# Stores on another issuing queue, the last two query tiles loaded a batch ahead and weighted by ScalarE, attention tiles at odd slots, one token sum later

## The chip, the cores and the metric

The kernel runs on one core of a Trainium2 chip. The metric is device microseconds of one execution. A profiled execution gives a span of its own, about 2 us shorter than the timed median (before: span 314.5 us, median 316.5 us), so spans are compared with spans and medians with medians.

## The reference

Linear attention with a cosine weighting feeds a gated feed-forward block (FFN):

```python
# 8 batches, 8 heads, 576 positions, head size 64
r   = max(x, 0); phi(x) = concat[r * cos(theta_s), r * sin(theta_s)]      # for q and k
kv  = einsum('bhsf,bhsd->bhfd', phi(k), v);  z = phi(k).sum(axis=2)
att = (phi(q) @ kv) / (phi(q) . z + 1e-6)                                 # 4608 tokens x 512
out = (silu(att @ w_gate) * (att @ w_val)) @ w_out                        # d_ff = 1536, float32 out
```

## The kernel before: the parts that matter

The tokens are worked off in nine groups (0 to 8) of 512. A group has 16 slots: twelve blocks of the FFN, then four of the output product. TensorE runs through these in order; everything else (the attention of the next batch, loads, transposes, stores) is hung into slots behind the TensorE work. Groups 7 and 8 (`GATE`) use a seven-product scheme for the gate, groups 2 to 8 for the output; such a scheme needs sums of operands, made by VectorE (`token_sum`, S1 to S4). A few more names: a bank is an accumulation buffer that TensorE writes; m and b are two partial products of the gate's scheme, which VectorE adds; C11 to C22 are the quarters of the output; an attention tile is made by matmuls of phit and kv and then three VectorE steps, den, rec and x.

```python
rel  = ctx.enter_context(tc.tile_pool(name="rel", bufs=1))     # r_q: ONE buffer
rawq = ctx.enter_context(tc.tile_pool(name="rawq", bufs=3))    # q as loaded
obp  = ctx.enter_context(tc.tile_pool(name="obp", bufs=2))     # output tiles
...
def phi_q(b, g):                        # relu on ScalarE, both weights in one multiply on VectorE
    if g == 0:
        st[b, "q"] = rel.tile([P, G, NC, 2, D], BF16, name="r_q")
    o = raws[b, "q"][:, g]
    relu_op("act", o, o)
    nc.vector.tensor_tensor(out=st[b, "q"][:, g], in0=o.unsqueeze(2).to_broadcast([P, NC, 2, D]),
                            in1=tab, op=ALU.mult)

def qturn_dma(b, e):                    # r_q is transposed by two DMA transposes into phit
    if e == 0:
        phit[b] = phip.tile([P, 2, G, NC, SH], BF16, name="phit")
    nc.sync.dma_start_transpose(out=phit[b][:, e]..., in_=st[b, "q"][e * SH:(e + 1) * SH]...)

def x_turn(t):                          # activations of an attention tile, also by DMA transpose
    nc.sync.dma_start_transpose(out=xT_of(t), in_=st["x", t])

def store(t, cols=slice(0, d_model), queues=None):
    for e in range(2):                  # two stores a tile, both on SyncE
        (queues or (nc.sync, nc.sync))[e].dma_start(out=out_v[...], in_=ob_of(t)[e * SH:(e + 1) * SH, cols])

def load_behind(b):                     # GpSimd loads a batch once phit of the one before is there
    nc.gpsimd.tensor_copy(out=hold2, in_=phit[b - 1][0:1, :, 0, 0, 0])
    load(b, "q")
    if b > 3:
        load_kv(b)
...
for b in range(2, B):                   # the plan: batch b is prepared in group b-2 and b-1
    s0 = SLOTS * (b - 1); p0 = s0 - SLOTS
    steps  = [lambda: phi_q(b, g) for g in range(G)]
    steps += [lambda: (relu_k(b, g, g + 1, keng), vmul(b, g)) for g in range(G)]
    fs, tq = [p0 + 12, p0 + 12] + [p0 + 11 + i for i in range(2, 8)], (p0 + 15, p0 + 16)
    at(p0 + 3 if b < 5 else p0 + 1, lambda: load_behind(b))
    ...
for t in ...:                           # the four attention tiles of the next group: their slots
    s = SLOTS * (tg - 1) + ((1, 2, 7, 9) if tg < 6 else (1, 2, 4, 7) if tg < 8 else (1, 2, 5, 6))[i]
    at(s, lambda: a_tile2(t), turn(t))  # (if tg - 1 in GATE)
```

Of the kernel before, what the change touches and what calls it, by code (L numbers as in the profile page):

```python
# [11 lines left out]
BF16 = mybir.dt.bfloat16  # L12
# [6 lines left out]
def kernel(  # L19
# [10 lines left out]
    nc = tc.nc  # L30
    B, H, S, D = q.shape
    P = 128
# [16 lines left out]
    HT = T // 2  # L49
    HD = d_model // 2  # L50
    KH = KC // 2
    GATE = (7, 8)

    consts = ctx.enter_context(tc.tile_pool(name="consts", bufs=1))
# [222 lines left out]
    def phi_q(b, g):  # L277

        if g == 0:
# [3 lines left out]
        nc.vector.tensor_tensor(out=st[b, "q"][:, g], in0=o.unsqueeze(2).to_broadcast([P, NC, 2, D]),  # L283
                                in1=tab, op=ALU.mult)

    def vmul(b, g):
        nc.vector.tensor_tensor(  # L287
            out=v2s[b == 1][:, g, :, :, 0:D],
            in0=(first if b == 0 and g == 0 else {"v": raw_of(b, "v")})["v"][:, g].unsqueeze(2).to_broadcast([P, NC, 2, D]),
            in1=tab, op=ALU.mult,  # L290
        )
# [59 lines left out]
    def kv_out2(b):  # L351

        ps = st[b, "kvps"][:, :, 0:4 * J * D1 // 2].rearrange("p e (j w x) -> p e j w x", j=J, w=2)
        for w, eng in enumerate((nc.scalar.copy, nc.vector.tensor_copy)):
            for i in range(2):
                eng(out=kv2s[b % 2][w * D:(w + 1) * D, :, :, i], in_=ps[i * D:(i + 1) * D, :, :, w])

# [249 lines left out]
    def ffn_by_quarters(tg, slot_of):  # L607

        B11, B12, B21, B22 = x_parts(tg)
        val, gates, count = {}, {}, [0]  # L610

        def bank(nm, **kw):
            return take(1, ("g", tg, nm), **kw).rearrange("p (i x) -> p i x", i=2)

        def free(nm):
            give_back(("g", tg, nm))

        def product(to, u, a, x, first):
            for i in range(2):
                for c in range(KH):  # L620
                    nc.tensor.matmul(out=to[:, i], lhsT=a[:, c, 2 * u + i], rhs=x[:, :, c],  # L621
                                     start=first and i == 0 and c == 0, stop=c == KH - 1, skip_group_check=True)

        def silu(u, w, j, src):
            if (u, w) not in gates:
                gates[u, w] = sg2p.tile([P, 2, T], BF16, name="sg2")
            nc.scalar.activation(out=gates[u, w][:, :, j * HT:(j + 1) * HT], in_=src, func=AF.Silu, scale=DOWN)  # L627

        def V(u, i, w):
            fc = 4 * u + 2 * i + w  # L630
            val[u, i, w] = take(1, ("v", tg, fc), fills=True)
            for kc in range(KC):
                nc.tensor.matmul(out=val[u, i, w], lhsT=wv_sb[:, kc, fc * P:(fc + 1) * P], rhs=xT[tg][:, :, kc],  # L633
                                 start=(kc == 0), stop=(kc == KC - 1))

        def mul(u, i, w):
            fc = 4 * u + 2 * i + w
            nc.vector.tensor_tensor(out=ht[:, fc], in0=gates[u, w][:, i], in1=val.pop((u, i, w)), op=ALU.mult)  # L638
            give_back(("v", tg, fc))

        def done():
            slot_of(count[0])
            count[0] += 1

        for u in range(3):
            a = bank("a", fills=True)
            product(a, u, A11, B11, True)
            b = bank("b", seeded=True)
            nc.scalar.copy(out=b, in_=a)
            e = bank("e", fills=True)  # L650
            product(e, u, W3, X3, True)
            m7 = m7p.tile([P, 2, HT], FP32, name="m7")
            nc.scalar.copy(out=m7, in_=e)
            free("e")
            V(*((u - 1, 1, 1) if u else (u, 0, 0)))
            done()
            product(b, u, W2, X2, False)
            c = bank("c", seeded=True)
            nc.vector.tensor_tensor(out=c, in0=m7, in1=b, op=ALU.add)
            product(a, u, A12, B21, False)  # L660
            silu(u, 1, 0, a)
            free("a")
            if u:
                mul(u - 1, 1, 1)
            V(u, 0, 0) if u else V(u, 1, 0)
            done()
            product(b, u, W1, X1, False)
            nc.vector.tensor_tensor(out=m7, in0=m7, in1=b, op=ALU.add)
            silu(u, 0, 1, m7)
            product(c, u, A22, X4, False)  # L670
            silu(u, 0, 0, c)
            free("c")
            V(u, 1, 0) if u else V(u, 0, 1)
            done()
            if u == 2:
                for n in (1, 2):
                    token_sum(n, 0, 4)
            mul(u, 0, 0)
            mul(u, 1, 0)
            if u == 2:  # L680
                token_sum(3, 4, 6)
            product(b, u, W4, B22, False)
            silu(u, 1, 1, b)
            free("b")
            if u:
                V(u, 0, 1)
            mul(u, 0, 1)
            if u:
                done()
                token_sum(*((3, 0, 4) if u == 1 else (4, 0, 4)))  # L690
        V(2, 1, 1)
        mul(2, 1, 1)
        for n in (1, 2):
            token_sum(n, 4, 6)
        done()
# [12 lines left out]
    def store(t, cols=slice(0, d_model), queues=None):  # L708
        for e in range(2):
            idx = 2 * t + e  # L710
            (queues or (nc.sync, nc.sync))[e].dma_start(out=out_v[idx // NC, idx % NC][:, cols],
                                                        in_=ob_of(t)[e * SH:(e + 1) * SH, cols])
# [40 lines left out]
    def token_sum(n, lo, hi):  # L753
        o, x, y, op = {
            3: (S3, aq[:, 0, 0], aq[:, 0, 1], ALU.subtract),
            1: (S1, aq[:, 0, 1], aq[:, 1, 1], ALU.add),
            2: (S2, S1, aq[:, 0, 0], ALU.subtract),
            4: (S4, aq[:, 1, 0], S2, ALU.subtract),
        }[n]
        nc.vector.tensor_tensor(out=o[:, lo:hi], in0=x[:, lo:hi], in1=y[:, lo:hi], op=op)  # L760
# [6 lines left out]
    def out_by_quarters(tg, slot_of):  # L767

        last = tg == NTG - 1
        t0 = tg * OUT  # L770
        for t in (t0, t0 + 2):
            ob_of(t)
# [41 lines left out]
        product(b, S2, T2, False)  # L814
        for p_, o_, x_ in each(b, c[0], C22):
            nc.vector.scalar_tensor_tensor(out=o_, in0=x_, scalar=UP, in1=p_, op0=ALU.mult, op1=ALU.add)
        token_sum(4, 4, 6)
        slot_of(0)
        product(a, aq[:, 1, 0], bq[:, 1, 0], False)
        copied("act", C11, a)  # L820
# [12 lines left out]
        if last:  # L833
            store_two(t0 + 2, slice(0, HD))
        else:
            for t in (t0 + 2, t0 + 3):
                store(t)
        slot_of(2)
        product(b, S4, bq[:, 1, 1], False)
        copied("dve", C12, b)  # L840
        free("b", nb)
        for t in (t0, t0 + 1):
            store(t, *((slice(HD, d_model), (nc.sync, nc.scalar)) if last else ()))
        slot_of(3)


# [149 lines left out]
    def load_behind(b):  # L996

        nc.gpsimd.tensor_copy(out=hold2, in_=phit[b - 1][0:1, :, 0, 0, 0])  # L998
        load(b, "q")
        if b > 3:  # L1000
            load_kv(b)

    def load_kv(b):
        for nm in ("k", "v"):
# [13 lines left out]
    for b in range(2, B):  # L1018
        s0 = SLOTS * (b - 1)
        keng = "dve" if b == 2 else "act"  # L1020
        steps = [lambda b=b, g=g: phi_q(b, g) for g in range(G)]
        steps += [lambda b=b, g=g: (relu_k(b, g, g + 1, keng), vmul(b, g)) for g in range(G)]
        if b == 2:
            fs, tq = [s0 + i for i in (0, 0, 1, 1, 4, 5, 5, 6)], (s0 + 2, s0 + 2)
        else:
            p0 = s0 - SLOTS
            fs, tq = [p0 + 12, p0 + 12] + [p0 + 11 + i for i in range(2, 8)], (p0 + 15, p0 + 16)
            if b == 3:
                fs, tq = [p0 + 12 + i for i in range(4)] + [s0 + 4, s0 + 4, s0 + 5, s0 + 5], (s0 + 2, s0 + 2)
            at(p0 + 3 if b < 5 else p0 + 1, lambda b=b: load_behind(b))  # L1030
        tk = (s0 + 4, s0 + {2: 8, 3: 7}.get(b, 5))
        for s, f in zip(fs, steps):
            at(s, f)
        for e in range(2):
            at(tq[e], lambda b=b, e=e: qturn_dma(b, e))
        at(tk[-1], lambda b=b: kv_mm(b), lambda b=b: kv_out2(b))
        at(tk[-1] + 1, lambda b=b: kv_free(b))
    for t in range(2 * OUT, NTG * OUT):
        tg, i = divmod(t, OUT)
        s = SLOTS * (tg - 1) + (5 if tg > 2 else 4) + 2 * i  # L1040
        if t == 2 * OUT:
            at(s, a_(t, 0))
            at(s + 1, a_(t, 1), turn(t))
        elif tg == 2:
            at((9, 10, 11)[i - 1] + SLOTS, lambda t=t: a_tile2(t), turn(t))
            if i == 2:
                at(11 + SLOTS, load_3)
        else:
            if t in (13, 14, 15):
                s = SLOTS * 2 + t - 4  # L1050
            elif tg - 1 in GATE:
                s = SLOTS * (tg - 1) + ((1, 2, 7, 9) if tg < 6 else (1, 2, 4, 7) if tg < 8 else (1, 2, 5, 6))[i]
            at(s, lambda t=t: a_tile2(t), turn(t))
    for tg in range(1, NTG):
        s0 = SLOTS * tg
# [46 lines left out]
```

## Time and profile before

| | before |
|---|---|
| timed, median (4 runs) | 316.53 us (316.38 to 317.22) |
| profiled span | 314.5 us |
| TensorE busy | 307.5 us (98%) |
| start of group 1 (first gate product) | 53.84 us |
| groups 1 to 8, us | 33.68, 32.62, 32.39, 32.74, 32.39, 32.43, 30.87, 29.00 |
| last matmul to end | 4.52 us |

A group's length is the distance of the first gate products of two neighbouring groups in the trace, so a wait at a group's start counts in the group before. Where this document says in which group time went, it compares these lengths.

### The profile page before, as it was taken

The page shows a single profiled execution, that of the slowest core. Times are in us where ns is not written, and L with a number is a line of the kernel's source. Part 1 is how long each engine was busy: PE and PEld are TensorE (multiplying, and loading weights), DVE is VectorE, ACT ScalarE, POOL GpSimd, SP SyncE. Part 2 cuts the span into 40 slices and gives each one's busy share as a digit, 9 for nine tenths or more (in the row PEclk, how much of TensorE's full clock was granted, in tenths as well). Part 3 has the DMA queues.
Part 4 walks back from the last instruction along what each step waited for, and adds up shares of the span by engine and source line. Part 5 has one row for each costly group of instructions (what it writes and reads, how often), then busy time and mean ns, then how long its engine had stood idle before and what let it go on. Part 6 is the DMA issues. An engine that isn't in the chain of part 4 may idle for free.

```text
span 314.5 us, 6775 instructions
## 1 busy us (share of the span) xinstructions
PE 307.5 (98%) x2696; PEld 189.7 (60%) x2696; DVE 228.2 (73%) x458; ACT 143.4 (46%) x264; POOL 36.0 (11%) x62
## 2 busy tenths in 40 slices
PE   8899999999999999999999999999999999999994
PEld 4597455455444585548654764577456866687673
DVE  7873777697678888587748786778779478946772
ACT  7554545763335346334543454335533345324530
POOL 7855102000200200030003000300000000000000
PEclk9999999999999999999999999999999999999999
DMA  7999999996897994989495979598951160014004
GB/s 268 217 198 197 206 205 138 226 133 99 143 208 114 150 145 110 148 119 196 100 153 75 200 144 154 73 192 135 164 86 35 40 145 17 20 38 98 0 2 133
DMA packets 74767, 41.07 MB, mean 131 GB/s; under 512 B 49904, under 2 KB 69872, under 8 KB 74736
## 3 DMA queue, kind: packets, MB, share of 16 engines
q1 hardware_dynamic: 51952, 22.55, 38.0%
q0 software_dynamic: 22192, 17.57, 37.2%
q10 hardware_dynamic: 592, 0.52, 0.5%
q8 instruction: 21, 0.34, 0.4%
q14 instruction: 10, 0.08, 0.1%
HBM read 37.75 MB, written 9.44 MB: 150 GB/s over the span
## 4 chain that ended last, share of the span: by engine, by line
PE 91%; DVE 5%; ACT 2%; issue 1%; ACTq 0%
PE banks L564 46%; PE banks L786 20%; PE banks L729 6%; PE banks L633 5%; PE banks L621 5%; PE banks L333 3%; PE banks L448 3%; DVE ht L638 1%; PE banks L494 1%; PE banks L430 1%; DVE v L287 1%; DVE sums L760 1%; DVE x L471 1%; PE banks L197 1%; PE banks L536 0%
## 5 line engine op out<-in xcount | busy, mean ns | idle before, releaser
L564 PE MATMUL banks<-xT,wg_sb 128*128 128x512 f16 (+2 forms) x368 | 86.6, 360 | 0.0
L564 PE MATMUL banks<-xT,wv_sb 128*128 128x512 f16 (+2 forms) x368 | 86.6, 360 | 0.0
L570 ACT ACTIVATE sg<-banks 128x512 bf16<-128x512 f32 (+2 forms) x92 | 51.5, 560 | 76.0 <-PE banks L564 74.0
L575 DVE TENSOR_TENSOR ht<-sg,banks 128x512 f16<-128x512 bf16 (+2 forms) x92 | 57.9, 637 | 29.7 <-PE banks L564 22.7
L564 PEld LDWEIGHTS <-wv_sb 128*128 128x128 f16 x368 | 35.5, 98 | 37.4
L564 PEld LDWEIGHTS <-wg_sb 128*128 128x128 f16 x368 | 33.9, 98 | 31.5 <-issue 0.2
L786 PEld LDWEIGHTS <-ht 128*128 128x128 f16 x336 | 32.5, 98 | 4.2
L786 PEld LDWEIGHTS <-sums 128*128 128x128 f16 x252 | 24.5, 98 | 4.2 <-issue 0.8
L633 PE MATMUL banks<-xT,wv_sb 128*128 128x512 f16 x96 | 24.3, 379 | 0.0
L283 DVE TENSOR_TENSOR r_q<-raw_q,tab 128x1152 bf16<-128x1152 bf16 x24 | 17.6, 754 | 7.4 <-ACT raw_q L266 7.1
L729 PE MATMUL banks<-wo_sb,ht 128*128 128x512 f16 x96 | 22.7, 379 | 0.0
L471 DVE TENSOR_TENSOR x<-banks,rec 128x512 f16<-128x512 f32 (+1 forms) x32 | 21.6, 674 | 1.3 <-PE banks L430 0.3
L786 PE MATMUL banks<-wo_sb,ht 128*128 128x256 f16 x168 | 20.6, 273 | 0.0
L287 DVE TENSOR_TENSOR v<-raw_v,tab 128x1152 bf16<-128x1152 bf16 x27 | 19.9, 751 | 0.5 <-ACT raw_v L849 0.5
L786 PE MATMUL banks<-wt_sb,sums 128*128 128x256 f16 x168 | 19.8, 273 | 0.1
L786 PE MATMUL banks<-wt_sb,ht 128*128 128x256 f16 x168 | 19.5, 273 | 0.0
L799 ACT ACTIVATE ob<-banks 128x512 f32<-128x512 f32 x14 | 8.4, 597 | 21.9 <-PE banks L786 21.9
L638 DVE TENSOR_TENSOR ht<-sg,banks 128x512 f16<-128x512 bf16 x24 | 15.5, 681 | 2.4 <-ACT sg L627 2.4
L266 ACT ACTIVATE raw_k<-raw_k 128x576 bf16<-128x576 bf16 (+1 forms) x25 | 17.1, 694 | 0.0
L998 POOL COPY hold<-phit 1x2 bf16<-1x2 bf16 x5 | 1.4, 287 | 129.3 <-DMA phit<-r_q 129.3
L760 DVE TENSOR_TENSOR sums<-ht 128x1024 f16<-128x1024 f16 (+1 forms) x28 | 15.5, 553 | 0.4
L266 ACT ACTIVATE raw_q<-raw_q 128x576 bf16<-128x576 bf16 x24 | 15.4, 675 | 0.0
(121 smaller groups left out, 334.6 us busy)
## 6 DMA issues: line engine op xcount, KB each, us to landing
out_dram<-ob SPq DMA_DIRECT2D x67, 128.0 KB, 2.5
raw_k<-in_k_dram POOLq DMA_DIRECT2D x7, 576.0 KB, 8.8
raw_q<-in_q_dram POOLq DMA_DIRECT2D x6, 576.0 KB, 6.0
raw_v<-in_v_dram POOLq DMA_DIRECT2D x6, 576.0 KB, 11.4
wo_sb<-in_moe_w_out_dram POOLq DMA_DIRECT2D x3, 512.0 KB, 12.8
wg_sb<-in_moe_w_gate_dram POOLq DMA_DIRECT2D x5, 256.0 KB, 9.4
wv_sb<-in_moe_w_val_dram POOLq DMA_DIRECT2D x5, 256.0 KB, 9.5
wo_sb<-in_v_dram SPq DMA_DIRECT2D x2, 576.0 KB, 4.0
```

The source lines that it names most:

```text
L266: nc.scalar.activation(out=out, in_=in_, func=AF.Relu)
L283: nc.vector.tensor_tensor(out=st[b, "q"][:, g], in0=o.unsqueeze(2).to_broadcast([P, NC, 2, D]), in1=tab, op=ALU.mult)
L287: nc.vector.tensor_tensor(out=v2s[b == 1][:, g, :, :, 0:D], in0=(first if b == 0 and g == 0 else {"v": raw_of(b, "v")})["v"][:, g].unsquee ...
L471: nc.vector.tensor_tensor(out=st["x", t].rearrange("p (y e d) -> p e y d", e=2, d=D)[:, :, ys], in0=ps[:, :, 0:2 * J * D1].rearrange("p e ...
L564: nc.tensor.matmul(out=st["f", tg, fc, lo][i], lhsT=(wg_sb, wv_sb)[i][:, kc, fs], rhs=xT[tg][:, ts, kc], start=(kc == 0), stop=(kc == KC - 1))
L570: nc.scalar.activation(out=sg[:, 0:n], in_=st["f", tg, fc, lo][0], func=AF.Silu, scale=DOWN)
L575: nc.vector.tensor_tensor(out=ht[:, fc, r:r + n], in0=st.pop(("s", tg, fc, lo))[:, 0:n], in1=ps[1], op=ALU.mult)
L633: nc.tensor.matmul(out=val[u, i, w], lhsT=wv_sb[:, kc, fc * P:(fc + 1) * P], rhs=xT[tg][:, :, kc], start=(kc == 0), stop=(kc == KC - 1))
L638: nc.vector.tensor_tensor(out=ht[:, fc], in0=gates[u, w][:, i], in1=val.pop((u, i, w)), op=ALU.mult)
L729: nc.tensor.matmul(out=o_ps[t], lhsT=ht[:, fc, r:r + P], rhs=wo_sb[:, fc], start=(fc == 0), stop=(fc == FC - 1))
L760: nc.vector.tensor_tensor(out=o[:, lo:hi], in0=x[:, lo:hi], in1=y[:, lo:hi], op=op)
L786: nc.tensor.matmul(out=to[i][:, 0] if len(to) == 2 else to[0][:, i], lhsT=a[:, kc, i * P:(i + 1) * P], rhs=b[:, kc], start=first and kc == ...
```

## The change

The intent: SyncE's queue, which carries the transposes TensorE depends on, is freed of stores; q of batches 6 and 7 is loaded a batch ahead, so that it can be turned earlier; VectorE is relieved of weighting it; and VectorE sums that sit just ahead of a TensorE product are moved away from it.

```diff
+    PHI_ACT = 6
+    def phi_q_part(b, c, w):                          # relu(x * w) = relu(x) * w, w = cos or sin >= 0
+        if (b, "q") not in st:
+            st[b, "q"] = rel.tile([P, G, NC, 2, D], BF16, name="r_q")
+        nc.scalar.activation(out=st[b, "q"][:, :, c, w], in_=raws[b, "q"][:, :, c], func=AF.Relu,
+                             scale=csk[:, c, w:w + 1])
 ... ffn_by_quarters: the last sum of the gated groups goes behind the output's start
-                token_sum(*((3, 0, 4) if u == 1 else (4, 0, 4)))
+            if u == 1:
+                token_sum(3, 0, 4)
 ... out_by_quarters
+        queues = (nc.gpsimd, nc.gpsimd) if tg > 2 else None
-        token_sum(4, 4, 6)
+        token_sum(4, 0 if tg in GATE else 4, 6)
-                store(t)
+                store(t, queues=queues)               # and the second pair of stores alike
 ... load_behind
-        load(b, "q")
+        if b < PHI_ACT:
+            load(b, "q")
         if b > 3:
             load_kv(b)
+        if PHI_ACT <= b + 1 < B:
+            load(b + 1, "q")
 ... the plan
-        steps = [lambda b=b, g=g: phi_q(b, g) for g in range(G)]
+        steps = [lambda b=b, g=g: phi_q(b, g) for g in range(G)] if b < PHI_ACT else []
+            if b >= PHI_ACT:
+                for c in range(NC):
+                    at(p0 + 4 + c, lambda b=b, c=c: (phi_q_part(b, c, 0), phi_q_part(b, c, 1)))
+                fs, tq = [p0 + 12, p0 + 12, p0 + 13, p0 + 15], (p0 + 13, p0 + 13)
 ... the attention tiles' slots
-            elif tg - 1 in GATE:
-                s = SLOTS * (tg - 1) + ((1, 2, 7, 9) if tg < 6 else (1, 2, 4, 7) if tg < 8 else (1, 2, 5, 6))[i]
+            elif tg in GATE:
+                s = SLOTS * (tg - 1) + ((1, 3, 7, 9) if tg < 6 else (1, 3, 5, 7))[i]
```

More of the change, by code (lines that the diff above doesn't have):

```diff
@@ L353, in kv_out2 @@
         ps = st[b, "kvps"][:, :, 0:4 * J * D1 // 2].rearrange("p e (j w x) -> p e j w x", j=J, w=2)
-        for w, eng in enumerate((nc.scalar.copy, nc.vector.tensor_copy)):
+        for w, eng in enumerate((nc.scalar.copy, nc.scalar.copy if b - 1 in GATE else nc.vector.tensor_copy)):
             for i in range(2):
@@ L842, in out_by_quarters @@
         for t in (t0, t0 + 1):
-            store(t, *((slice(HD, d_model), (nc.sync, nc.scalar)) if last else ()))
+            store(t, *((slice(HD, d_model), (nc.sync, nc.scalar)) if last else (slice(0, d_model), queues)))
         slot_of(3)
```

## The prediction

> **What bounds the kernel now.** I read the engine shares and the chain that ended last on the profile's page, then TensorE's waits, then the timeline around the stages that the change touches.
>
> ```profile
> PE 307.5 (98%) x2696; PEld 189.7 (60%) x2696; DVE 228.2 (73%) x458; ACT 143.4 (46%) x264; POOL 36.0 (11%) x62
> PE 91%; DVE 5%; ACT 2%; issue 1%; ACTq 0%
> 54.00:310.00 256.00, 255.34 (x2153) 157.21 (x2150) 189.64 (x353) 112.90 (x201) 12.68 (x21) 1.00 0.67 115
> ```
>
> The third line is the stretch view from 54 to 310 us (columns: PE, weight loads, DVE, ACT, POOL, granted clock, DMA share): TensorE is busy for 255.34 of 256.00 us at full clock. It is the bound, so ACT (112.9) or DVE (189.6) work is worth nothing in itself; only TensorE's gaps are. A busy share can hide small ones, so I took the distance of neighbouring matmul starts in the trace less the streaming time of the columns (213 ns for 512, seen all through the FFN, in proportion for fewer). After 100 us the gaps over 60 ns are: 0.20 us before the last output product of each of groups 2 to 5; 0.12 us at 185.28, the start of group 5; in group 7 0.51 (257.20), 0.24 (267.65), some 0.15 (263 to 265) and 0.24 us (274.84); 0.13 us at 303.68 in group 8; and pairs of 0.10 us where the small attention matmuls begin and end, which no reordering removes. **All that this change could win is some 2.3 us, 0.7%.** The program order confirms that no TensorE instruction is added or dropped; five attention tiles only move.
>
> **What the skill says.** (1) The Trainium skill, "ScalarE: Activation LUTs", section "What ACT_TABLE_LOAD costs": an activation takes 186 ns plus 0.833 ns an element, some 93 ns more for a per-partition pointer operand, and neighbours overlap by 93 ns. The trace agrees: 675 ns for 576 columns (formula 666), 475 ns for 260 columns with a pointer scale (496). (2) "DMA: Bandwidth & Descriptors", section "Issuing engines are not separate DMA queues": another issuing engine only saves sequencer time; the 16 DMA engines are shared. (3) The same page, section "SWDGE vs HWDGE vs iDMA": GpSimd's and SyncE's transfers feed different queues of each DMA engine, which takes turns. The trace agrees: activation transposes that land 2.4 us after issue with nothing beside them (255.47 to 257.91) take 8 to 9 us while GpSimd's loads run (203.25 to 211.84).
>
> **The change, part by part.**
>
> Stores on GpSimd: 40 stores (groups 3 to 7) leave SyncE, where a group's eight held the queue 5 to 6 us. GpSimd's issues cost 0.74 us each, 30 us in 190, on an engine idle otherwise. An output buffer is wanted some 25 us later. Directly worth 0. Indirectly, the transpose of r_q no longer waits behind stores.
>
> ScalarE weighting (batches 6 and 7): four relus (675 ns) and four DVE multiplies (754 ns) go; 18 activations of 256 columns with a pointer scale come. Each: 186 + 93 + 213 = 0.49 us, 0.40 us in a row; the traced 475 ns less overlap gives 0.38. A pair costs 0.85 us a slot. With the SiLU (0.60 us) that is 1.45 of the 1.73 us that TensorE spends on a slot. In total ACT gains 2 x (18 x 0.40 - 2.7) = 9 us and DVE loses 6 us, beside TensorE. The multiplies' places before the output's last product are filled by three v multiplies of the same length, so the 0.20 us gaps stay.
>
> Token sum S4 moved behind the output's start: 0.68 us of DVE leaves the front of the S2 sum, for which TensorE waits 0.24 and 0.13 us: -0.37 us.
>
> Tiles at odd slots: in group 7 the second of two neighbouring tiles leaves slot 2, where TensorE waited for its bank:
>
> ```profile
> 256.46 0.69 DVE L471 TENSOR_TENSOR x<-banks,rec 128x512 f16<-128x512 f32 x1
> 257.20 0.60 PE L621 MATMUL banks<-kvt,wgs_sb 128*128 128x256 f16 x4 [0.35 <-DVE x L471]
> ```
>
> But at slots 3 and 7 its 1.1 us of DVE (den 0.17, rec 0.20, x 0.69) stands just before the sum of m and b that TensorE needs two products later. By hand this leaves some 0.3 us a time. Of 0.90 us of gaps I take 0.4 as saved.
>
> q a batch ahead: q of 6 goes behind group 3's loads, some 3.4 us more transfer (k to v there: 146.36 to 149.78), ending near 153.2. That group's last activation transposes landed at 149.99 and 150.58, with the loads; they would now land near 153.5 to 154, and group 4 (152.54) wants them: about 1 us. In group 4 load and transposes start earlier, which frees the 0.12 us at 185.28.
>
> **The wait that I expect to decide.** r_q has one buffer. ScalarE may write batch 6 into it only when both transposes of batch 5 have read it; in the new program the first of the 18 waits for them. It stands after group 4's fifth SiLU:
>
> ```profile
> 152.44 0.76 DVE L283 TENSOR_TENSOR r_q<-raw_q,tab 128x1152 bf16<-128x1152 bf16 x1 [1.26 <-ACT raw_q L266]
> 157.79 7.62 SPq L306 DMA_TRANSPOSE phit<-r_q  x2
> 160.57 0.60 ACT L570 ACTIVATE sg<-banks 128x512 bf16<-128x512 f32 x1 [1.19 <-PE banks L564]
> 167.89 0.42 PE L448 MATMUL banks<-kv,phit 128*128 128x65 bf16 x8
> 169.65 0.18 POOL L998 COPY hold<-phit 1x2 bf16<-1x2 bf16 x1 [31.01 <-DMA phit<-r_q]
> ```
>
> r_q of batch 5 is full at 153.20; its transposes start at 157.79, behind the stores, and are done at 169.5, 11.7 us later (10.1 to 12.0 us over the five pairs). ScalarE would be there at 161.2. Without stores ahead the pair starts at 153.3, and ends at L = 165.0; sharing the DMA engines with the group's stores, now on the other queue (a store is 64 packets of 2 KB at 115 ns, 0.46 us of 16 engines; some five or six more now overlap the pair), L is nearer 167.4. ScalarE is in order, so SiLU 5 and the kv copies wait with it. From L: two activations 0.85, SiLU to 1.35, kv copies on ACT to 2.0 and on DVE to 3.0, then den, rec and x of tile 20 to 4.1. Tile 21 takes tile 20's banks (the program's bank order says so), so TensorE starts it no earlier than L + 4.15. It started at 167.89: **TensorE loses L - 163.74, thus 1.3 us for L = 165.0 and 3.7 for 167.4.** The later conditions (block 7's value bank, free at L + 2.1 and wanted at 167.02; block 8's, free at L + 4.8 and wanted at 169.01) are milder. The 1 us at group 4's start lies inside this loss, as r_q does not move with it. For batch 7 the transposes begin at slot 13 of group 4 and end some 5 us before that threshold of group 5: no loss there.
>
> Sum: gains 0.37 + 0.4 + 0.12 = 0.9 us; loss about 2.7 us (between 1.3 and 3.7, weighted to the later); net +1.8: 316.58 + 1.8 = **318.4 us**.
>
> **Rivals.** (a) The transposes are early enough, or stores leave enough room: the loss is only group 4's late activations or nothing, and the kernel is 0 to 0.9 us faster, 315.7 to 316.6. For it: DMA share over 151.8 to 157.8 was 0.60, so there is room, and two of five pairs took 10.1 us. Against it: share 0.93 as soon as transposes run. (b) GpSimd's in-order queue becomes the bound: stores wait for the hold on phit, buffers come late. Against it: each hold (group 4, slot 1) stands after the previous group's stores, and output buffers have 25 us. It would be worth over 3 us a group, 330 us; 2%. (c) ScalarE becomes the bound in slots 4 to 12 even without the wait (pair slower than 0.85 us, being four runs of 64). 1.45 of 1.73 leaves 0.28 a slot; a pair of over 1.1 us would cost TensorE some 0.1 to 0.3 us a slot in two groups, 319 to 321 us. (d) The transposes are slowed as far as the loads slow theirs: L near 169.5, loss 5.8 us, 321.5 us.
>
> **Range and chances.** Low end: rival (a) whole, 315.6. High end: L = 168.5, or (c), 320.6. Faster by over 2% would need 6.3 us where TensorE has 2.3 to give: 0.005. Slower by over 2% needs (b) or more than (d): 0.025.
>
> **What would show it.** Right: before the first r_q activation in group 4, ScalarE waits 3 to 7 us for the transposes phit<-r_q; TensorE shows a gap of 1 to 4 us between 163 and 170 (bank of x or ht); r_q activations near 0.47 us; the transposes of batch 5 issued at 153.3; group 7 near 30.2 us against 30.9, and the gap before S2 gone. Wrong: no such ScalarE wait, or one below 2.5 us with TensorE streaming on (rival a); GpSimd stores issued long after their ob is ready (b); activations over 0.55 us (c). The prediction fails most likely through L: the duration of a transpose pair beside stores on another queue is the one number that nothing in this trace shows.

## The result, and the profile after

The changed kernel took **320.18 us** (median of 4 runs, 319.71 to 320.46) against 316.53 us before. The ratio is 1.0109, 95% interval 1.009 to 1.0128: slower by 1.1%. (A ratio here is the mean time of one kernel's runs over that of the other's of the same rounds, so not quite the ratio of the medians.) The profiled span went from 314.5 to 318.4 us.

The page of the kernel after, engine shares and the chain that ended last:

```profile
PE 306.2 (96%) x2696; PEld 189.5 (60%) x2696; DVE 223.0 (70%) x448; ACT 152.9 (48%) x292; POOL 56.8 (18%) x102
PE 84%; DMA 5%; DVE 4%; SPq 3%; ACT 2%; issue 1%; ACTq 0%
```

TensorE has the same 2696 products and fewer busy microseconds in a longer span: the time went into waiting. DMA and SPq (SyncE's queue), absent from the chain before, now hold 8% of it.

TensorE's waits between 54 and 312 us, kernel after (us in total, times, the longest); before, this view has one line, the 0.3 us at the value x that the prediction shows:

```profile
PE banks L571 <- DMA xT<-x: 1.2, 1, 1.2
PE banks L455 <- DVE x L478: 0.9, 1, 0.9
PE banks L628 <- DVE banks L666: 0.6, 2, 0.4
PE banks L571 <- ACT sg L577: 0.5, 1, 0.5
```

Three of the four stand within 17 us of each other. The timeline of the kernel after there (start, duration, engine, line, what it writes and reads, in brackets the idle time before and what ended it):

```profile
152.79 0.76 DVE L284 TENSOR_TENSOR r_q<-raw_q,tab 128x1152 bf16<-128x1152 bf16 x1 [1.26 <-ACT raw_q L267]
154.12 10.81 SPq L313 DMA_TRANSPOSE phit<-r_q  x2
154.25 1.04 PE L571 MATMUL banks<-xT,wg_sb 128*128 128x512 f16 x4 [1.20 <-DMA xT<-x]
...
167.14 0.91 ACT L290 ACTIVATE r_q<-raw_q,cs_all 128x256 bf16<-128x256 bf16 x2 [4.25 <-DMA phit<-r_q]
168.58 1.02 PE L571 MATMUL banks<-xT,wg_sb 128*128 128x512 f16 x4 [0.53 <-ACT sg L577]
170.62 0.69 DVE L478 TENSOR_TENSOR x<-banks,rec 128x512 f16<-128x512 f32 x1
171.36 0.42 PE L455 MATMUL banks<-kv,phit 128*128 128x65 bf16 x8 [0.90 <-DVE x L478]
```

Read from below: the matmuls of an attention tile start at 171.36, held by x, which VectorE made late, because ScalarE stood for 4.25 us before its first r_q activation, because the second transpose of the old r_q was only done then (its last packets landed at 166.91). The other loss, at 154.25, is TensorE waiting for the activations of group 4: their last transpose landed at 154.21, with the load of q of batch 6 (landed 153.90) added to that group's transfers; in the kernel before the last one had landed at 150.58.

| | before | after | difference |
|---|---|---|---|
| start of group 1 | 53.84 | 54.20 | +0.36 |
| groups 1, 2, 6 | 33.68, 32.62, 32.43 | 33.67, 32.62, 32.43 | 0.0 |
| group 3 | 32.39 | 33.75 | +1.36 |
| group 4 | 32.74 | 34.20 | +1.46 |
| group 5 | 32.39 | 32.22 | -0.17 |
| groups 7 and 8 | 30.87, 29.00 | 30.88, 28.86 | -0.13 |
| last matmul to end | 4.52 | 5.50 | +0.98 |
| span | 314.49 | 318.36 | +3.87 |

Group 3's +1.36 is the wait at 154.25 (a gap of 1.37 us in the distances of matmul starts). Group 4's +1.46 is a gap of 0.70 at 168.58 and one of 1.06 at 171.36, less 0.12 and 0.20 of gaps that went. The start of group 1 lies between 53.8 and 54.4 us over all profiled kernels here, so +0.36 is not put down to the change.

### The profile page after: what moved, and what is told of

Read it like the earlier page. It is cut to its first block, busy times and chain, and to the rows that moved or that the text cites. A ratio compares the mean times of both kernels' runs of the same rounds, so it can differ in the third digit from the quotient of the medians.

```text
span 318.4 us, 6799 instructions
## 1 busy us (share of the span) xinstructions
PE 306.2 (96%) x2696; PEld 189.5 (60%) x2696; DVE 223.0 (70%) x448; ACT 152.9 (48%) x292; POOL 56.8 (18%) x102
## 4 chain that ended last, share of the span: by engine, by line
PE 84%; DMA 5%; DVE 4%; SPq 3%; ACT 2%; issue 1%; ACTq 0%
PE banks L571 41%; PE banks L795 20%; PE banks L737 6%; PE banks L640 5%; PE banks L628 4%; DMA ht<-in_k_dram 3%; PE banks L340 2%; PE banks L455 2%; DMA phit<-r_q 2%; SPq L313 2%; DVE ht L645 1%; DVE x L478 1%; PE banks L501 1%; SPq L161 1%; PE banks L437 1%
## 5 line engine op out<-in xcount | busy, mean ns | idle before, releaser
L719 POOL DMA_DIRECT2D out_dram<-ob x40 | 20.9, 531 | 108.3 <-ACT ob L808 108.3
L808 ACT ACTIVATE ob<-banks 128x512 f32<-128x512 f32 x14 | 8.4, 597 | 20.9 <-PE banks L795 20.7
L290 ACT ACTIVATE r_q<-raw_q,cs_all 128x256 bf16<-128x256 bf16 x36 | 16.1, 498 | 4.3 <-DMA phit<-r_q 4.3
```

The source lines that it names most:

```text
L290: nc.scalar.activation(out=st[b, "q"][:, :, c, w], in_=raws[b, "q"][:, :, c], func=AF.Relu, scale=csk[:, c, w:w + 1])
L719: (queues or (nc.sync, nc.sync))[e].dma_start(out=out_v[idx // NC, idx % NC][:, cols], in_=ob_of(t)[e * SH:(e + 1) * SH, cols])
```

## The experiments

All were correct, with five rounds. The kernel before had a median of 316.64 us beside experiments 1 to 8 and of 316.70 beside 9 and 10. Experiments 1 to 4 and 8 alter the changed kernel, 5 to 7 put one part alone on the kernel before, and 9 and 10 build a better kernel.

**My theory** after the result: the single buffer of r_q costs the 1.76 us in group 4 (write-after-read, ScalarE held), the longer load the 1.37 us before it. **Rivals**: ScalarE is simply too slow with 18 activations in these slots; or the stores on GpSimd's queue are what slows things.

### 1. r_q of batch 6 gets a home of its own

If the activations write memory that no transpose reads, the wait is gone; nothing else about them changes. The memory is that of the gate's weight sums, three of which are then made one to three groups later.

```diff
-            st[b, "q"] = rel.tile([P, G, NC, 2, D], BF16, name="r_q")
+            st[b, "q"] = rq_own if b == 6 else rel.tile([P, G, NC, 2, D], BF16, name="r_q")
+    rq_own = wgs_sb.rearrange("p n c u x -> p (n c u x)")[:, 3072 // 2:].bitcast(BF16).rearrange(...)
-        at(SLOTS * (1 + n * (GATE[0] - 1) // 4) + FC + 3, lambda n=n: gate_weight_sum(n))
+        at(SLOTS * (1, 5, 5, 6)[n] + FC + 3, lambda n=n: gate_weight_sum(n))
```

> The changed kernel, but r_q of batch 6 has a place of its own (in the gate weight sums' tile, three of whose sums are made later), so ScalarE need not wait for batch 5's transposes. My theory (two delays in series on one path: the activation transposes of group 4 that land late behind the added q load, 1.37 us, and on top of them the wait for r_q up to L - 163.74): the gaps of 0.70 and 1.06 us go, the 1.37 us at group 4's start stays, and a new wait doesn't come, so some 1.8 us faster than the changed kernel, 318.4 us. Rival 'ScalarE's 18 activations are too much for slots 4 to 12': gaps of 1 us or more stay between group 4's slots 5 and 12, under 0.7 us gained, 319.5 or more.

Measured: **318.07 us** (317.68 to 319.0), ratio to before 1.0053 (1.004 to 1.0067). Group 4 fell from 34.20 to 32.46 us, by 1.74: the whole 1.76 us. Its first activations run with no wait in front:

```profile
162.89 0.90 ACT L290 ACTIVATE wgs_sb<-raw_q,cs_all 128x256 bf16<-128x256 bf16 x2
```

This clears ScalarE: it does all 18 activations of 498 ns in the same slots, and TensorE loses nothing. The wait at group 4's start stays (group 3: 34.15), 0.40 longer in this profile. The edit has a small cost of its own, a gap of 0.42 us in group 7, where the last moved weight sum now runs, and it also took 0.85 us off the time after the last matmul, which experiment 8 explains. None of these three had been expected, so that the total came so near the expected 318.4 is luck; the length of group 4 is the evidence.

### 2. q of batch 5 loaded ahead as well

If the late activations at group 4's start come from q of batch 6 loading beside them, then giving that group one load fewer (its own q, a batch earlier) should remove the wait.

```diff
-        if b < PHI_ACT:
+        if b < PHI_ACT - 1:
             load(b, "q")
...
-        if PHI_ACT <= b + 1 < B:
+        if PHI_ACT - 1 <= b + 1 < B:
             load(b + 1, "q")
```

> The changed kernel, but q is loaded a batch ahead from batch 5 on, so group 2 (whose transposes land 1.5 to 3 us before they are needed) takes one load more and group 3 no more than before. My theory: the gap of 1.37 us at group 4's start goes, but ScalarE still waits for r_q until about the same L, so TensorE waits the more at tile 21 and nearly nothing is gained: 319.7 to 320.3 (the transposes may start 0.5 us earlier and run faster, as the load is out of their way; every us off L is a us gained). Rival 'the gaps are independent and add up': 1.4 us gained, 318.8.

Measured: **323.35 us** (321.93 to 325.84), ratio 1.0222 (1.0184 to 1.026). I missed. Group 3 was indeed clean (32.39), but the extra load fell into group 2, whose last activations then landed at 122.21 and held group 3 back (group 2: 34.39, +1.77). The wait had only moved one group forward. And group 4 became 39.35 us: the pair of transposes of batch 5 was issued at 155.96 and landed at 171.0, 15.0 us beside stores that ran from 154 to 166, so ScalarE was freed later still, TensorE waited 4.3 us, and a stretch of half clock came with it (see experiment 4).

### 3. Both

```diff
+            st[b, "q"] = rq_own if b == 6 else rel.tile([P, G, NC, 2, D], BF16, name="r_q")   # and the rest of 1
+        if b < PHI_ACT - 1:                                                                # and the rest of 2
```

> The changed kernel with both: r_q of batch 6 in a place of its own, and q ahead from batch 5 on. My theory: all of group 4's 3.1 us is gone, 317.0 us; what then is left over the kernel before is what the last stage added in the profile (1.0 us) less some 0.5 us of small gains. Rival 'stores on GpSimd cost by themselves (contention, descriptor writing)': stays at 318.5 or more.

Measured: **318.14 us** (316.8 to 318.32), ratio 1.0039 (1.0024 to 1.0055), a miss by 1.1 us. Groups 3 and 4 are clean (32.39 and 32.45), as expected, but group 2 is 34.22, with a wait of 1.60 us that I had not counted. That agrees with the reading of 2: in both of these groups the wait for activations came with the additional 0.6 MB of q; the r_q wait is separate from it.

### 4. The stores back on SyncE

```diff
-        queues = (nc.gpsimd, nc.gpsimd) if tg > 2 else None
+        queues = None
```

> The changed kernel with all stores on SyncE's queue as before. My theory: batch 5's transposes then start behind eight stores, near 158, and end near 170, so L is 3 us later and TensorE loses about 3 us more in group 4: 323 us. Rival 'the stores on GpSimd are what slows, by sharing the DMA engines with the transposes': the pair runs faster without them and the time is that of the changed kernel or lower, 318 to 320.

Measured: **323.04 us** (320.84 to 324.45), ratio 1.0186 (1.0157 to 1.0215). The number is the expected one, in part by luck: the half clock below was not foreseen, and the time after the last matmul fell by 0.82 us (experiment 8). The pair now stands behind eight stores: issued 159.22, landed 171.04. It takes 11.8 us there, as in the kernel before, but ends 4.1 us later than in the changed kernel. The stores on GpSimd are therefore no culprit; without them the r_q wait is far worse. Kernel of experiment 4, timeline of ScalarE and TensorE:

```profile
171.28 0.91 ACT L290 ACTIVATE r_q<-raw_q,cs_all 128x256 bf16<-128x256 bf16 x2 [8.00 <-DMA phit<-r_q]
172.72 1.76 PE L571 MATMUL banks<-xT,wg_sb 128*128 128x512 f16 x4 [4.28 <-ACT sg L577]
```

Group 4 took 38.56 us, 6.1 more than in experiment 1, where it has no such wait. The wait itself is a gap of 4.44 us. The stretch view shows the rest (after the window and its length, busy us of PE, weight loads, DVE, ACT and POOL with their counts, then the granted clock, the DMA share and GB/s):

```profile
168.10:172.60 4.50, 0.34 (x2) 0.06 (x1) 0.00 (x0) 1.32 (x4) 1.05 (x3) 1.00 0.17 25
172.72:176.20 3.48, 3.48 (x12) 1.38 (x12) 3.17 (x7) 3.44 (x9) 1.23 (x2) 0.52 0.92 134
```

After the wait TensorE is busy for all 3.48 us at a granted clock of 0.52; its products of 512 columns start 427 ns apart instead of 213. Half of that stretch is lost, an estimate of 1.7 us, and 4.44 + 1.7 is the 6.1. In experiment 2, TensorE worked for 5.3 us at half clock after its wait of 4.32 us. Waits of up to 1.77 us, of which these runs have several, were followed by full clock. The Trainium skill, "TensorE: Matmul & The Clock Gate", section "Part 1: The HAM clock gate (the "warmup" mystery)", describes this: half rate after an idle window of some 3.4 us, full rate again after as much sustained work, 426.7 ns between starts of 512 columns while cold. The trace of experiment 4 agrees: its clock record has half rate for 3.41 us. In experiment 2 that record has 6.83 us, from 171.19, when TensorE was still waiting, so the way back took longer there than the 3.4 us of sustained work.

### 5. The token sum alone, on the kernel before

```diff
-                token_sum(*((3, 0, 4) if u == 1 else (4, 0, 4)))
+            if u == 1:
+                token_sum(3, 0, 4)
...
-        token_sum(4, 4, 6)
+        token_sum(4, 0 if tg in GATE else 4, 6)
```

> The kernel before with the token sum S4 of the gated groups moved behind the output's start, and nothing else. My theory: the waits of 0.24 us (group 7) and 0.13 us (group 8) before the S2 product go, no other comes, 0.35 us faster (316.2). Rival: S4, now 1536 wide and later, is late for its own product: a gap of 0.1 us or more before the last product of group 7 or 8, and no gain.

Measured: **316.05 us**, ratio 0.9985 (0.997 to 0.9999). Group 7 became 30.61 (-0.26), group 8 28.86 (-0.14). The prediction's -0.37 for this part was right.

### 6. The odd slots alone, on the kernel before

```diff
-            elif tg - 1 in GATE:
-                s = SLOTS * (tg - 1) + ((1, 2, 7, 9) if tg < 6 else (1, 2, 4, 7) if tg < 8 else (1, 2, 5, 6))[i]
+            elif tg in GATE:
+                s = SLOTS * (tg - 1) + ((1, 3, 7, 9) if tg < 6 else (1, 3, 5, 7))[i]
```

> The kernel before with the tiles of groups 7 and 8 made at odd slots, and nothing else. The prediction had a saving of 0.4 us; the changed kernel's trace has group 7's gaps of 0.24, 0.55 and 0.39 us, each ended by VectorE's sum of m and b. Theory now: the odd slots put a tile's den, rec and x right ahead of that sum, so the three gaps come from the odd slots alone: group 7 is 0.2 to 0.4 us longer than before, 316.8. Rival: they come from the token sum's move, and here group 7 is shorter than before by 0.4.

Measured: **316.82 us**, ratio 1.0007 (0.9994 to 1.002). The interval includes no change at all, so the finding rests on the trace: group 7 became 31.12 us, **0.25 longer**, and its gaps of 0.24, 0.54 and 0.39 us are those of the changed kernel and of experiments 1 to 4 and 8, which all have the odd slots. (Group 4 was 0.33 longer in this profile, from activations that landed 0.33 us later at its end; the edit does not touch that group.) The tile's arithmetic now stands before the sum of m and b that TensorE waits for. Timeline of experiment 6:

```profile
259.67 0.69 DVE L471 TENSOR_TENSOR x<-banks,rec 128x512 f16<-128x512 f32 x1
260.28 0.69 DVE L659 TENSOR_TENSOR banks<-m,banks 128x512 f32<-128x512 f32 x1
261.02 0.60 PE L621 MATMUL banks<-kvt,wgs_sb 128*128 128x256 f16 x4 [0.38 <-DVE banks L659]
```

and the same triple in the kernel after:

```profile
262.17 0.69 DVE L478 TENSOR_TENSOR x<-banks,rec 128x512 f16<-128x512 f32 x1
262.78 0.69 DVE L666 TENSOR_TENSOR banks<-m,banks 128x512 f32<-128x512 f32 x1
263.52 0.60 PE L628 MATMUL banks<-kvt,wgs_sb 128*128 128x256 f16 x4 [0.38 <-DVE banks L666]
```

In both the multiply of x ends as the sum begins, and TensorE's product follows the sum's end: a wait of 0.38 us, in another place than before. In experiment 6 the gaps of group 7's gate products are 0.24, 0.54 and 0.39 us, in place of 0.51, 0.24 and 0.15 before: 1.17 against 0.90, near the 0.25 by which the group grew.

### 7. The stores on GpSimd alone, on the kernel before

```diff
+        queues = (nc.gpsimd, nc.gpsimd) if tg > 2 else None      # and store(t, queues=queues)
```

> The kernel before with the stores of groups 3 to 7 on GpSimd's queue, and nothing else. My theory: nothing waits for the transposes of r_q early in the next group, so nothing is lost or won beyond 0.3 us: 316.4 to 316.7; the transposes start 3 to 4 us earlier and land 2 to 3 us earlier. Rival 'stores on GpSimd cost by themselves' (descriptor writing, or the longer last stage seen in the changed kernel): 317.2 or more, with a gap of TensorE or a last stage over 5 us.

Measured: **316.17 us**, ratio 0.9988 (0.9975 to 1.0001). The wait of 0.12 us at group 5's start is gone in this profile, but that isn't credited to the stores: this wait is 0.45 us in experiment 6 and 0.31 in experiment 10, which has the same stores. How much earlier do the transposes of batch 5 come?

```profile
154.07 10.77 SPq L306 DMA_TRANSPOSE phit<-r_q  x2
```

They are issued at 154.07 instead of 157.79 and landed at 168.22 instead of 169.51. A start 3.7 us earlier gave a landing only 1.3 us earlier, where I had expected 2 to 3: beside stores on another queue the pair takes 14.15 us instead of 11.7. On the GpSimd side nothing queued up; in the kernel after its stores cost 531 ns of issue each and found the engine idle (an issue is not the transfer: these stores land after 4.8 us in the median, those on SyncE before after 2.5). The page's group (busy us and mean ns, then idle time before and what ended it):

```profile
L719 POOL DMA_DIRECT2D out_dram<-ob x40 | 20.9, 531 | 108.3 <-ACT ob L808 108.3
```

This refutes the prediction's rival (b), and the time, with a last stage of 4.53 us, refutes this experiment's rival. Half of the gap of 0.24 us at group 7's token sum was also gone here (0.12 is left); why, I did not find.

### 8. The time after the last matmul

The changed kernel ends 5.50 us after its last matmul, the kernel before 4.52, though the code there is the same. ScalarE's timeline before:

```profile
306.70 1.78 ACTq L718 DMA_DIRECT2D out_dram<-ob  x2
308.70 0.60 ACT L799 ACTIVATE ob<-banks 128x512 f32<-128x512 f32 x1 [2.02 <-PE banks L786]
```

and after:

```profile
309.59 2.94 ACTq L726 DMA_DIRECT2D out_dram<-ob  x2
312.58 0.60 ACT L808 ACTIVATE ob<-banks 128x512 f32<-128x512 f32 x1 [3.02 <-PE banks L795]
```

The first of these two store issues takes 2.23 us after and 0.74 before, and the next evacuation comes 1.0 us late. Inside it, at 310.0 us, the trace has one 8 KB packet of a DMA queue of kind "instruction". The packet doesn't name its engine; I take it for ScalarE's because in the kernel after and in experiments 2 and 8 alike it comes after 448 recorded ScalarE instructions (the kernel before has 425 in all). The theory: ScalarE, which has 28 instructions more than before, has to fetch its next piece of program just there. The rival: GpSimd's stores disturb the end. The test adds eight ScalarE instructions of no effect to the changed kernel, some 200 us earlier, so that the fetch comes earlier in the program:

```diff
+    for i in range(8):
+        at(SLOTS * 2 + 3 + i, lambda: nc.scalar.activation(out=tiny, in_=half_pi, func=AF.Silu))
```

> The changed kernel with 8 tiny activations (one column) more on ScalarE in group 2's idle time. In its trace ScalarE's first store of the last group takes 2.23 us to issue (0.74 in the kernel before), beside an 8 KB packet of the instruction queue that starts inside it, and the last stage is 1 us longer. Theory: ScalarE runs out of fetched instructions just there, because the added activations moved the boundary onto the store; 8 or more instructions ahead move it off again: the store issues in 0.74 us, last stage 4.5 to 4.7 us, 319.3 us. Rival: the long issue comes from the stores on GpSimd's queue, and stays: 320.2.

Measured: **318.91 us** (318.61 to 319.9), ratio 1.008 (1.0064 to 1.0095), against 1.0109 (1.009 to 1.0128) for the changed kernel: more instructions, and by the ratios 0.9 us less time; as the intervals overlap a little, the tail in the traces is the better evidence. The tail is 4.50 us, the packet comes at 307.0 in an idle stretch of ScalarE, and the issue is short again:

```profile
309.19 1.78 ACTq L726 DMA_DIRECT2D out_dram<-ob  x2
311.18 0.60 ACT L808 ACTIVATE ob<-banks 128x512 f32<-128x512 f32 x1 [2.02 <-PE banks L795]
```

The other runs agree. In experiment 2, whose ScalarE program is the changed kernel's, the packet falls into the first store's issue again (at 315.6; tail 5.53). In experiments 1, 3 and 4 it comes at one of the later stores, and the tail is 4.60 to 4.68, which accounts for experiment 1's 0.85 us. In the kernel before the last such packet is at 272.6. The count of these packets is on the pages, before and then after:

```profile
q14 instruction: 10, 0.08, 0.1%
```

```profile
q14 instruction: 11, 0.09, 0.1%
```

So the longer tail comes from where in ScalarE's program a fetch falls, and thus from the number of its instructions, not from the stores on GpSimd: in this program eight more are cheaper than none.

### 9. The parts that help

The kernel before, with the token sum of 5, the stores of 7, and one thing that the changed kernel showed by accident: in groups 4 and 5 the 0.20 us wait before the output's last product had vanished (see below), so here VectorE's multiplies of r_q are moved away from that product in groups 2 to 5.

```diff
-            fs = [p0 + 12, p0 + 12] + [p0 + 11 + i for i in range(2, 8)]
+            fs = [p0 + 12, p0 + 12, p0 + 14, p0 + 14] + [p0 + 11 + i for i in range(4, 8)]
```

> The kernel before with the two parts that helped by themselves (token sum late, stores on GpSimd) and the third and fourth r_q multiply of batches 4 to 7 one slot later, behind VectorE's last update of C22, so that the 0.20 us gap before the last output product of groups 2 to 5 should go. By the gaps: 0.37 + 4 x 0.20 + 0.12 (start of group 5) = 1.3 us faster than the kernel before, 315.3. Rival: the multiplies one slot later hold up the copy of C12 and with it the next group's bank or the transposes: a new gap at the group's start and no gain beyond 0.5.

Measured: **315.53 us** (315.08 to 315.97), ratio 0.9961 (0.9946 to 0.9975). The 0.20 us gaps of groups 2 to 5 are gone, and no new gap came: 1.2 us gained of the 1.3 expected.

### 10. Attention tiles out of the gated groups

As 9, but the tiles for groups 7 and 8 go where VectorE has room: those of 7 to slots 1, 3, 5, 7 of group 6, those of 8 to slots 9 and 11 of group 6 and 1 and 5 of group 7.

```diff
-            elif tg - 1 in GATE: ...
+            elif tg == 7:
+                s = SLOTS * 6 + (1, 3, 5, 7)[i]
+            elif tg == 8:
+                s = (SLOTS * 6 + 9, SLOTS * 6 + 11, SLOTS * 7 + 1, SLOTS * 7 + 5)[i]
```

> As e9, and group 6, which has TensorE gaps nowhere, makes two of group 8's four tiles (tiles of group 7 at slots 1, 3, 5, 7, of group 8 at 9 and 11), so that group 7 keeps one tile at slot 1 and one at slot 5, ahead of no sum of m and b. The gaps of 0.51 and 0.24 us in group 7 should go: 0.6 us faster than e9, 314.7. Rival: VectorE in group 6 becomes too full and TensorE waits there: group 6 longer by more than the 0.5 us that the two tiles' own matmuls take.

Measured: **314.59 us** (314.44 to 314.81), ratio 0.9933 (0.9921 to 0.9945). Group 6 grew by 0.51 (the moved products themselves), group 7 fell from 30.62 to 29.45. The view of TensorE's waits from 54 to 312 us lists none, but that view leaves out small ones: by the distances of matmul starts, 0.24 us are left in group 7 (at 255.93, at another product) and 0.31 at group 5's start, where TensorE, now earlier, waits for activations that landed at 184.94. This beats both kernels: 2 us better than before, 5.6 better than the change.

## Why the prediction was right or wrong

The time lies inside the range (320.18 in 315.6 to 320.6), but the rise of 3.65 us is twice the 1.8 predicted. The range's high end had been drawn for a late L (the time at which the old r_q has been read) or a slow ScalarE; what took the time so near it was mainly the slots and the end of the kernel, so that the range held is in part luck. The terms, predicted and measured on the spans:

| term | predicted | measured | from |
|---|---|---|---|
| token sum | -0.37 | -0.40 | experiment 5 |
| tiles at odd slots | -0.4 | +0.25 | experiment 6 |
| wait at group 5's start | -0.12 | -0.12 | distances of matmuls in the kernel after |
| r_q wait, with the late activations inside it | +2.7 | +3.13 | gaps 1.37, 0.70, 1.06; experiments 1 and 3 |
| 0.20 us gaps of groups 4 and 5 | 0 | -0.37 | distances of matmuls |
| after the last matmul | 0 | +0.98 | experiment 8 |
| start of group 1 | 0 | +0.36 | differs between profiles |
| sum | +1.8 | +3.8 (span +3.87) | |

- **The deciding wait: right.** ScalarE waited 4.25 us for the transposes of batch 5 (predicted 3 to 7), and tile 21's products, at 171.36, were the last thing held. Experiment 1 removes the wait by removing its cause. L was predicted almost exactly: it was 166.91, and as this profile runs 0.36 us late from group 1 on, 166.55 in the time of the kernel before, against the 166.4 that the point implies. For that L the formula L - 163.74 gives 2.81 us; the gaps add up to 3.13. The missing 0.3 is the way from L to TensorE, 4.45 us where 4.15 had been summed by hand: ScalarE's first activation began 0.23 us after the landing. (Put in without the shift, 166.91 gives 3.17, which agrees only because the two differences cancel.) What was named as least known, a transpose pair beside stores on another queue, did vary most: 12.8, 14.15 and 15.0 us in three kernels, against 11.7 behind them.
- **Late activations at group 4's start: right in mechanism.** Predicted about 1 us, measured 1.37; and it did lie inside the L term: the two later gaps, 1.76 us, are what the 3.13 leaves after it.
- **ScalarE fast enough: right.** 498 ns each against 470 to 490 predicted, a pair 0.91 against 0.85; rival (c) is refuted by experiment 1. The page's group after:

```profile
L290 ACT ACTIVATE r_q<-raw_q,cs_all 128x256 bf16<-128x256 bf16 x36 | 16.1, 498 | 4.3 <-DMA phit<-r_q 4.3
```

- **The step that failed: "Of 0.90 us of gaps I take 0.4 as saved".** I had seen that the tile's 1.1 us of VectorE would stand before the sum of m and b, had put its leftover at 0.3 us a time, and still counted a gain. Experiment 6 shows a loss of 0.25: the waits that came cost more than the ones that went. Group 7 stayed at 30.88 instead of 30.2.
- **A gain missed: "so the 0.20 us gaps stay".** They went in groups 4 and 5. I had taken three v multiplies for the same length as three of r_q; the third r_q one starts at 182.44, when ScalarE's relu that feeds it has just ended (182.41), 0.16 us later than right behind the second; the v ones follow each other. Before and after, the multiplies and the output step behind them:

```profile
180.94 2.26 DVE L283 TENSOR_TENSOR r_q<-raw_q,tab 128x1152 bf16<-128x1152 bf16 x3
183.11 0.68 DVE L827 SCALAR_TENSOR_TENSOR ob<-banks,ob 128x512 f32<-128x512 f32 x1
```

```profile
184.41 2.09 DVE L294 TENSOR_TENSOR v<-raw_v,tab 128x1152 bf16<-128x1152 bf16 x3
186.41 0.68 DVE L836 SCALAR_TENSOR_TENSOR ob<-banks,ob 128x512 f32<-128x512 f32 x1
```

  The run of three is 0.17 us shorter, which is nearly the gap. That timing is read from the traces, not tested by itself; experiment 9 shows that taking VectorE work from that place removes the gap.
- **A cost not thought of: the end, +0.98.** The prediction took the code after the last matmul as untouched, which it is; its instruction fetch was not.
- **Slips in the working.** The gaps listed add up to 2.19 us, not 2.3. GpSimd's 0.74 us is the issue of a load; a store took 0.53. The 2 KB packets of stores took 139 ns in the mean in the groups concerned (130 over the whole run), not 115; and on GpSimd's queue a store is 32 packets of 4 KB, 310 ns each in the mean beside the pair.

The misses, +0.43 on the wait, +0.65 on the slots, +0.98 at the end and +0.36 at the start, less 0.37, are 2.05 of the 2.07 us by which the span's +3.87 exceeded +1.8. What stays open: how the stores' packets and the transposes share the DMA engines in detail, why a transpose pair took 12.8 us in one kernel and 15.0 in another, and why experiment 7 also lost half of the small gap of 0.24 us in group 7.

## What to carry to other kernels

Work moved earlier and to another engine can collide with the buffer of the batch before: ask who still reads the destination, when that reader ends, and what else waits on the engine that now stands in line. When the bound engine has almost no gaps, moving other work merely moves its wait (experiments 2 and 6), unless it goes to a place with slack (9 and 10). And look at the end of the kernel even when its code is unchanged.

## What the Trainium skill lacked or had wrong

- "Runtime: NRT & Kernel Launch", section "Instruction fetch mechanics", calls the cost of crossing an instruction block "mostly hidden". Here one 8 KB fetch fell into ScalarE's store issue near the end, which took 2.23 us instead of 0.74, and the kernel ended 1.0 us later; eight idle instructions placed earlier undid it (tail 5.50 to 4.50 us). The advice to look for a fetch in the last microseconds is missing.
- "DMA: Bandwidth & Descriptors", section "Latency and other measured facts", gives 261 GB/s for a DMA transpose with a non-contiguous middle dimension. The pair here moves r_q, 128 x 4608 elements of two bytes, 1.18 MB; 11.7 us from issue to landing is 101 GB/s, an estimate from these two numbers; all but the first 1.4 us had hardly another transfer beside it. The page's figure is that of one kernel, so this is a second case rather than a refutation.
- No page that I read gives what such a transpose loses beside plain stores of another queue: 12.8 to 15.0 us a pair, against 11.7 and 11.8 behind them in one queue. In experiment 7, starting 3.7 us earlier made it land 1.3 us earlier.
- The same page, section "Anatomy of one DMA — SWDGE (gpsimd) path", calls the generation of descriptors "small, variable" and gives no number for it. Here an issue of a 128 KB store held GpSimd for 0.53 us (20.9 us for 40); how much of that is descriptors, no run shows.
